# The second MoE's steps get a row count, six of them with a last tile of 64 rows, and attention by pairs starts two tiles later

## The chip, the cores and the metric

The kernel runs on one core of a Trainium2 chip. The metric is the device time of one execution in microseconds (us). TensorE (PE) multiplies matrices, VectorE (DVE) and ScalarE (ACT) work on tiles, GpSimd (POOL) does so too and issues the indirect transfers, SyncE (SP) issues the other transfers. PEld in a profile is PE's loading of the stationary operand.

## The reference

Chunked attention over 4 x 768 positions with 8 heads of 64, a dense gated MLP (called the first MoE here), and a top-1 mixture of 8 experts, all in float32:

```python
# attention: chunks of 32 queries, 16 positions of context to the left, 8 to the right, 8 memory slots
scores = scale * np.matmul(q_c, k_full.transpose(0, 1, 3, 2))
a = softmax(scores)
out[:, :, c_start:c_end] = np.matmul(a, v_full)
# first MoE: 3072 tokens x 512, d_ff 1536
g = x @ w_gate
x = silu(g) * (x @ w_val) @ w_out
# second MoE: w1 [8, 512, 1024], w2 [8, 1024, 512]
logits = x @ w_gate
e_idx = np.argmax(logits, axis=1)
for e in range(E):
    mask = e_idx == e
    h = np.maximum(x[mask] @ w1[e], 0.0)
    out[mask] = gate_w[mask, None] * eom[mask, e, None] * (h @ w2[e])
```

## The kernel before

Attention runs in 48 tiles of 64 queries. A list of pieces (`attention_pieces`) is dealt out over slots between the matmuls of the first MoE's first token groups, one group of 384 tokens for every six tiles. A single tile (`at_S`) adds the mask on PE, by a matmul with an identity (L354), then multiplies 128 query columns at a time with 96 keys (L357); DVE only takes the maximum. A pair of tiles (`at_S2`) multiplies 64 x 64 blocks (L386), DVE adds the mask to both halves (L391) and takes the maximum (L392); ACT then takes the exponentials of 16 heads in a row (L395). Tiles below `PAIRED` are single, the rest run in pairs. While this goes on, DVE also converts the first MoE's weights from their 64-bit form (L226 to L231).

The first MoE keeps 8 groups of 384 tokens times 12 slices of d_ff; every f32 factor is split into a high and a low half in fp32r (a reduced f32 that PE multiplies in one pass), and three products replace one. After each group its tokens are routed: logits, expert, position in the expert's table (`posi`), and a scatter of the token's number into the table.

The second MoE runs in steps. A step takes one expert and two or three tiles of 128 tokens. It goes through 8 chunks of the expert's weights, 128 of the 1024 hidden columns each. Per chunk, `split_chunk` makes the high and low halves (ACT the cast, DVE one half of the low part and POOL the other, L889: tiles `wh`/`wl` and `gvh`/`gvl` in turn), `mm1` runs twelve matmuls into `g` with the tokens as moving operand (L947), DVE and ACT make the two halves of `h` (L951, L953), and a chunk later `mm2` runs three matmuls per tile into `o` (L969), with 128 columns of `h` as the stationary operand and 512 output columns moving. `gather` fetches a step's tokens by index (L916), `prep_x` transposes them on PE (L934), `evac_y` scales the result and `scatter_y` writes it to the tokens' rows (L985).

Three steps come first, for experts 0, 1 and 2 and known beforehand. What the other steps take is computed on the chip by `make_schedule`: a generator on DVE over tiny rows of one partition (8 experts, 19 slots, 8 x 19 products), run piece by piece by `later(delay, ...)` at ticks of a clock that counts two ticks per chunk. Then follow five steps of three tiles and four of two, always run, and up to ten more of two tiles that run only if the schedule asks for them (`tc.If`). At chunk `ready` the first dynamic transfers are issued.

Of the kernel before, what the change touches and what calls it, by code (L numbers as in the profile page):

```python
# [21 lines left out]
def tile_chunk_attention_moe_moe2(  # L22
# [16 lines left out]
    nc = tc.nc  # L39
# [26 lines left out]
    NTRI = 5  # L66
    NPAIR = 14
    NPU = 4
    NCV = 6
    PAIRED = 2 * GU  # L70
    NSP = 31
    WARM = 10
    LOADS = "w0 q0 q1 q2 w1 v0 v1 q3 w2 q4 w3 w4 v2 w5 q5 v3 v4 v5"
# [662 lines left out]
        nc.vector.tensor_scalar(out=out_, in0=a, scalar1=s1, scalar2=s2, op0=op0, **kw)  # L736

    def row(tag, shape=(1, E), dtype=F32):
        return sm.tile(list(shape), dtype, tag=tag, name=tag)

    def stt(out_, a, s1, b, op0, op1):
        nc.vector.scalar_tensor_tensor(out=out_, in0=a, scalar=s1, in1=b, op0=op0, op1=op1)

    def make_schedule():
        NS = NTRI + NPAIR

        def over_slots(vec, n):
# [22 lines left out]
        stt(tri_, hf, 1.0, odd, ALU.is_ge, ALU.mult)  # L770
        m8 = row("m8", (1, E, E))
        tt(m8, over_slots(tri_, E), upto, ALU.mult)
        tcum = total(m8, E, "tcum")
        yield
        stt(tri_, tcum, float(NTRI), tri_, ALU.is_le, ALU.mult)
        ts(tcum, tcum, float(NTRI), ALU.min)
# [16 lines left out]
        gt = row("gt", (1, NTRI, E))
        tt(gt, over_slots(tcum, NTRI), over_experts(sidx[:, 0:NTRI], NTRI), ALU.is_le)
        te = total(gt, NTRI, "te")
        tt(pk, pk, skip, ALU.subtract)
        ts(pk, pk, 1.0, ALU.add, float(2 * P), ALU.mult)
        stt(pk, pe, float(ES), pk, ALU.mult, ALU.add)
# [3 lines left out]
        tt(gt, over_experts(te, NTRI), over_slots(sidx[:, 0:E], NTRI), ALU.is_equal)  # L802
        tt(gt, gt, over_slots(trow, NTRI), ALU.mult)
        tst = total(gt, NTRI, "tst")
        stt(pk[:, 0:NTRI], te, float(E), pk[:, 0:NTRI], ALU.is_ge, ALU.mult)
        stt(te, te, float(E), te, ALU.is_lt, ALU.mult)
        tt(pe[:, 0:NTRI], pe[:, 0:NTRI], te, ALU.add)
        yield
        stt(pk[:, 0:NTRI], tst, -2.0 * P, pk[:, 0:NTRI], ALU.add, ALU.max)
        ts(sched_i[:, 1, 0:NS], pk, float((E - 1) * ES + N), ALU.min)  # L810
        ts(sched_i[:, 0, 0:NS], pe, float(E - 1), ALU.min)
        tt(used, used, pcum[:, E - 1:E], ALU.add)
        ts(sched_i[:, 0, NS:NS + 1], used, float(NTRI), ALU.subtract, 0.0, ALU.max)


    steps = [(e, 2) for e in range(NEARLY)] + [(None, 3)] * NTRI + [(None, 2)] * NPAIR
# [357 lines left out]
```

## Time and profile before

| what | value |
| --- | --- |
| median of three runs | 1165.75 us (1165.01 to 1165.78) |
| profiled execution | 1161.31 us, span 1159.6 us |
| PE busy | 1112.3 us, 96% of the span |
| weight loads (PEld) busy | 992.8 us, 86% |
| DVE / ACT / POOL busy | 592.7 / 597.7 / 674.1 us |
| mean granted clock of TensorE | 0.984 of full |

A busy time is the sum of an engine's instructions; overlapping ones count once. Matmuls are pipelined: the length shown for one is longer than the distance from its start to that of the next, and the distance is what it costs. The table is one profiled execution; the median belongs to other executions.

### The profile page before, as it was taken

How to read it: one execution, taken by the hardware profiler on the slowest of the kernel's cores; microseconds unless marked ns; L12 is line 12 of the kernel's file. 1: busy time of each engine (PE TensorE's matmuls, PEld its weight loads, DVE VectorE, ACT ScalarE, POOL GpSimd, SP SyncE). 2: the span in 40 equal slices, each digit the busy share in tenths (PEclk: the TensorE clock that was granted, in tenths of full speed). 3: DMA queues.
4: the chain of work that ended last, by engine and by line, in shares of the span. 5: the costliest groups of instructions: out<-in, count | busy, mean ns of one | idle time of the engine just before them, and what ended most of it. 6: DMA issues, size and time to landing. Idle time of an engine off the chain costs nothing.

```text
span 1159.6 us, 20391 instructions
## 1 busy us (share of the span) xinstructions
PE 1112.3 (96%) x7458; PEld 992.8 (86%) x7458; DVE 592.7 (51%) x1167; ACT 597.7 (52%) x1300; POOL 674.1 (58%) x459
## 2 busy tenths in 40 slices
PE   7789899999999999999999999999999999999994
PEld 5678788898998998899899899888789998998994
DVE  6699844444444544544444443425884344444541
ACT  5678755545555556555554554444454434334551
POOL 4589854554654554555365565566666555566773
PEclk7799999999999999999999999999999999999998
DMA  9777524211211211221210100265169444546673
GB/s 207 193 196 214 165 59 124 53 27 36 63 37 37 60 42 29 52 49 29 58 40 18 38 12 19 67 125 173 64 213 324 157 147 158 171 156 197 206 227 123
DMA packets 204959, 126.55 MB, mean 109 GB/s; under 512 B 110960, under 2 KB 181744, under 8 KB 204850
## 3 DMA queue, kind: packets, MB, share of 16 engines
q1 hardware_dynamic: 199282, 110.70, 35.3%
q0 software_dynamic: 5568, 14.45, 3.6%
q8 instruction: 61, 1.00, 0.4%
q14 instruction: 48, 0.39, 0.2%
HBM read 111.61 MB, written 14.82 MB: 109 GB/s over the span
## 4 chain that ended last, share of the span: by engine, by line
PE 80%; DVE 6%; issue 4%; POOL 3%; SPq 2%; DMA 2%; ACT 2%; POOLq 0%; ACTq 0%; DVEq 0%
PE ps_g L530 32%; PE acc L571 15%; PE g L947 11%; PE o L969 11%; PE ps_pv L433 2%; PE ps_t L325 2%; PE ps_att L416 2%; SPq L274 1%; PE ps_att L386 1%; PE ps_x L616 1%; PE a L934 1%; DVE ps_c L228 1%; DVE ps_c L226 1%; PE ps_l L626 1%; DVE w L231 1%
## 5 line engine op out<-in xcount | busy, mean ns | idle before, releaser
L180 POOL TENSOR_TENSOR gvl<-w,gvh 128x1024 fp32r<-128x1024 f32 x96 | 233.1, 2429 | 89.9 <-ACT gvh L179 66.7
L530 PE MATMUL ps_g<-xh,gvh 128*128 128x384 f32 x768 | 271.7, 354 | 0.6 <-ACT gvh L179 0.6
L530 PE MATMUL ps_g<-xh,gvl 128*128 128x384 f32 x768 | 261.4, 340 | 3.5 <-POOL gvl L180 3.5
L530 PE MATMUL ps_g<-xl,gvh 128*128 128x384 f32 x768 | 261.5, 340 | 0.0
L180 POOL TENSOR_TENSOR ol<-w,oh 128x512 fp32r<-128x512 f32 x96 | 124.7, 1299 | 201.6 <-ACT oh L179 201.5
L571 PE MATMUL acc<-oh,h 128*128 128x512 f32 x576 | 202.9, 406 | 0.9 <-DVE h L560 0.9
L543 DVE SCALAR_TENSOR_TENSOR th<-th,ps_g 128x384 f32<-128x384 f32 x96 | 53.0, 552 | 194.1 <-ACT th L538 194.1
L530 PEld LDWEIGHTS ps_g<-xh,gvh 128*128 128x128 f32 x768 | 145.5, 189 | 5.2 <-ACT gvh L179 0.8
L530 PEld LDWEIGHTS ps_g<-xh,gvl 128*128 128x128 f32 x768 | 145.1, 189 | 4.5 <-POOL gvl L180 4.5
L530 PEld LDWEIGHTS ps_g<-xl,gvh 128*128 128x128 f32 x768 | 145.5, 189 | 1.8
L554 ACT CAST h<-th 128x384 fp32r<-128x384 f32 x96 | 49.1, 512 | 166.8 <-DVE th L552 166.7
L571 PEld LDWEIGHTS acc<-oh,h 128*128 128x128 f32 x576 | 108.1, 188 | 25.8 <-issue 1.4
L951 ACT ACTIVATE h<-g 128x256 fp32r<-128x256 f32 (+1 forms) x96 | 41.3, 430 | 160.4 <-PE g L947 151.4
L571 PE MATMUL acc<-ol,h 128*128 128x512 f32 x288 | 113.7, 395 | 0.3 <-POOL ol L180 0.3
L953 DVE SCALAR_TENSOR_TENSOR h<-g,h 128x256 fp32r<-128x256 f32 (+1 forms) x96 | 45.8, 477 | 118.3 <-ACT h L951 97.2
L560 DVE TENSOR_TENSOR h<-th,h 128x384 fp32r<-128x384 f32 x96 | 81.0, 844 | 39.1 <-ACT h L554 38.5
L179 ACT CAST gvh<-w 128x1024 fp32r<-128x1024 f32 x96 | 100.4, 1046 | 1.1 <-POOL w L234 1.1
L538 ACT ACTIVATE th<-ps_g 128x384 f32<-128x384 f32 x96 | 47.0, 490 | 92.8 <-PE ps_g L530 92.6
L552 DVE TENSOR_TENSOR th<-th,ps_g 128x384 f32<-128x384 f32 x96 | 53.0, 552 | 64.6 <-PE ps_g L530 64.0
L969 PE MATMUL o<-gvh,h 128*128 128x512 f32 x232 | 80.9, 397 | 1.6 <-DVE h L953 1.6
L969 PE MATMUL o<-wh,h 128*128 128x512 f32 x232 | 80.4, 394 | 0.0
L889 POOL TENSOR_TENSOR wl<-w,wh 128x512 fp32r<-128x512 f32 x30 | 50.6, 1690 | 37.6 <-ACT wh L887 37.1
(196 smaller groups left out, 2299.8 us busy)
## 6 DMA issues: line engine op xcount, KB each, us to landing
w<-in_moe_w_dram SPq DMA_DIRECT2D x120, 256.0 KB
ra<-in_moe_w_dram SPq DMA_DIRECT2D x72, 256.0 KB
kt<-in_k_dram SPq DMA_DIRECT2D x35, 176.0 KB
vt<-in_v_dram SPq DMA_DIRECT2D x35, 176.0 KB
xs<-xr SPq DMA_DIRECT2D x8, 769.5 KB
st<-in_moe_w_gate_dram SPq DMA_DIRECT2D x12, 512.0 KB
st<-in_moe_w_val_dram SPq DMA_DIRECT2D x12, 512.0 KB
st<-in_moe_w_out_dram SPq DMA_DIRECT2D x12, 512.0 KB
```

Of the source, the lines that this page charges most:

```text
L179: nc.scalar.copy(out=hi, in_=src)
L180: lo_eng.tensor_tensor(out=lo, in0=src, in1=hi.bitcast(F32), op=ALU.subtract)
L530: nc.tensor.matmul(ps, a[:, c], x[:, kk, :], start=(n == 0), stop=(n == 3 * KD - 1))
L538: nc.scalar.activation(out=th, in_=ps, func=AF.Tanh, scale=0.5)
L543: nc.vector.scalar_tensor_tensor(out=th, in0=th, scalar=1.0, in1=ps, op0=ALU.add, op1=ALU.mult)
L552: nc.vector.tensor_tensor(out=hh, in0=hh, in1=ps, op=ALU.mult)
L554: nc.scalar.copy(out=h1, in_=hh)
L560: nc.vector.tensor_tensor(out=h2, in0=hh, in1=h1.bitcast(F32), op=ALU.subtract)
L571: nc.tensor.matmul(accs[g][j], a[:, c], w_, start=(f == 0 and n == 0), stop=(f == NF - 1 and n == 2))
L889: eng.tensor_tensor(out=b[:, i], in0=r[:, i], in1=a[:, i].bitcast(F32), op=ALU.subtract)
L947: nc.tensor.matmul(ps, wx[:, 0, c * P:(c + 1) * P], xx[:, c, :], start=(i == 0), stop=(i == 3 * KD - 1))
L969: nc.tensor.matmul(ysd[s][t], hx[:, c], wx[:, 1], start=(j == 0 and i == 0), stop=(j == NFE - 1 and i == 2))
```

## The change

Steps carry a row count. After the three early steps come two three-tile steps with 384 rows, three with 320, one two-tile step with 256 and three with 192; the conditional ones keep 256. In the six narrow steps the last tile has 64 rows: its gather, transposes, scaling and scatter take 64, `mm1` has 320 or 192 moving columns, and `mm2` for that tile loads 64 stationary columns and still moves 512. `make_schedule` decides by the number of leftover blocks of 64 which expert's rest goes to a wide or a narrow step. It has 14 pieces in place of 7, one per tick in place of every second; `ready` goes from 14 to 15. Its row tiles have one buffer in place of two. `PAIRED` goes from 12 to 14.

```diff
     NPU = 4
+    NTW = 2
+    NPW = 1
     NCV = 6
-    PAIRED = 2 * GU
+    PAIRED = 2 * GU + 2
...
     def row(tag, shape=(1, E), dtype=F32):
-        return sm.tile(list(shape), dtype, tag=tag, name=tag)
+        return sm.tile(list(shape), dtype, tag=tag, name=tag, bufs=1)
...
+        def running(vec, tag):
+            m8 = row("m8", (1, E, E))
+            tt(m8, over_slots(vec, E), upto, ALU.mult)
+            return total(m8, E, tag)
...
-        hall, odd = hof[:, 0, :], hof[:, 1, :]
+        hall, odd, half = hof[:, 0, :], hof[:, 1, :], hof[:, 2, :]
         yield
+
         hf = row("hf")
         tt(hf, hall, early1, ALU.subtract)
+        t5 = row("t5")
+        stt(t5, hf, 1.0, odd, ALU.is_ge, ALU.mult)
+        t6 = row("t6")
+        tt(t6, t5, half, ALU.mult)
+        tt(t5, t5, t6, ALU.subtract)
+        c6 = running(t6, "c6")
...
+        ts(li, li, 1.0, ALU.add, float(2 * P), ALU.mult)
+        stt(li, le, float(ES), li, ALU.mult, ALU.add)
+        ge = row("ge", (1, NS, E))
+        tt(ge, over_slots(scum, NS), over_experts(si, NS), ALU.is_le)
+        se = total(ge, NS, "sse")
+        srow = row("srow")
+        tt(srow, hall, odd, ALU.add)
+        ts(srow, srow, 1.0, ALU.subtract, float(2 * P), ALU.mult)
+        tt(srow, srow, ebase[0:1, 0, :], ALU.add)
+        yield
+        ge = row("ge", (1, NS, E))
+        tt(ge, over_experts(se, NS), over_slots(sidx[:, 0:E], NS), ALU.is_equal)
+        tt(ge, ge, over_slots(srow, NS), ALU.mult)
+        pk = total(ge, NS, "pk")
+        off = row("off", (1, NS))
+        ts(off, se, float(E), ALU.is_ge, float(E * ES), ALU.mult)
+        tt(pk, pk, off, ALU.add)
+        yield
...
+        ts(sched_i[:, 1, 0:NS], pk, float((E - 1) * ES + N), ALU.min, 0.0, ALU.max)
+        ts(sched_i[:, 0, 0:NS], se, float(E - 1), ALU.min)
+        tt(b1, b1, scum[:, last], ALU.add)
+        ts(b1, b1, float(M), ALU.subtract)
+        tt(b0, lcum[:, last], lc, ALU.subtract)
+        tt(b1, b1, b0, ALU.max)
+        ts(sched_i[:, 0, NS:NS + 1], b1, float(NPU), ALU.add)
+
+
+    HALF = P // 2
+    steps = ([(e, 2, 2 * P) for e in range(NEARLY)]
+             + [(None, 3, 3 * P)] * NTW + [(None, 3, 3 * P - HALF)] * (NTRI - NTW)
+             + [(None, 2, 2 * P)] * NPW + [(None, 2, 2 * P - HALF)] * (NPU - NPW)
+             + [(None, 2, 2 * P)] * (NPAIR - NPU))
+
+    def rows(s, t):
+        return min(P, steps[s][2] - t * P)
...
         for t in range(steps[s][1]):
+            r = rows(s, t)
             nc.gpsimd.indirect_dma_start(
-                out=x[:, t, :], out_offset=None, in_=xs,
-                in_offset=bass.IndirectOffsetOnAxis(ap=idx[:, t:t + 1], axis=0))
+                out=x[0:r, t, :], out_offset=None, in_=xs,
+                in_offset=bass.IndirectOffsetOnAxis(ap=idx[0:r, t:t + 1], axis=0))
...
             sc = m2_tile(s, "sc")
-            nc.vector.tensor_copy(sc[:, 0:nt], x[:, 0:nt, DM:XW])
+            full = steps[s][2] // P
+            nc.vector.tensor_copy(sc[:, 0:full], x[:, 0:full, DM:XW])
+            if full < nt:
+                nc.vector.tensor_copy(sc[0:HALF, full:nt], x[0:HALF, full:nt, DM:XW])
...
         for c in range(KD):
-            nc.tensor.transpose(ps[:, c, :], x[:, t, c * P:(c + 1) * P], ident)
-        c_ = slice(t * P, (t + 1) * P)
-        hi_lo(ps, th[:, :, c_], tl[:, :, c_], nc.vector)
+            nc.tensor.transpose(
+                ps[:, c, 0:r], x[0:r, t, c * P:(c + 1) * P], ident[0:r, 0:r])
+        c_ = slice(t * P, t * P + r)
+        hi_lo(ps[:, :, 0:r], th[:, :, c_], tl[:, :, c_], nc.vector)
 
     def mm1(n):
         s = n // NFE
-        w = steps[s][1] * P
+        w = steps[s][2]
...
         for t in range(nt):
-            c = slice(t * P, (t + 1) * P)
+            r = rows(s, t)
+            c = slice(t * P, t * P + r)
             for i, (hx, wx) in enumerate(((h1, a), (h1, b), (h2, a))):
-                nc.tensor.matmul(ysd[s][t], hx[:, c], wx[:, 1],
+                nc.tensor.matmul(ysd[s][t][0:r], hx[:, c], wx[:, 1],
 
...
-        for i in range(7):
-            later(13 + 2 * i, next, sched, None)
+        for i in range(14):
+            later(13 + i, next, sched, None)
         nextc = NRA + NF
-        ready = 14
+        ready = 15
```

On DVE, in the second MoE between one `w*l` (the low half of a weight chunk) and the next `h`, the fourth gap of the schedule held six small instructions; `m`, `pk`, `te`, `trow` and the others are rows of the schedule. Before:

```order
L889 TENSOR_TENSOR wl<-w,wh 128x512
L640 TENSOR_TENSOR gt<-tcum,sidx 1x40
L643 TENSOR_REDUCE te<-gt 1x5
L640 TENSOR_TENSOR pk<-pk,skip 1x19
L736 TENSOR_SCALAR pk<-pk 1x19
L742 SCALAR_TENSOR_TENSOR pk<-pe,pk 1x19
L742 SCALAR_TENSOR_TENSOR trow<-hof,ebase 1x8
L953 SCALAR_TENSOR_TENSOR h_9396<-g,h_9394 128x256
```

The same gap of the changed kernel, without the `wl` ahead and the `h` behind:

```order
L738 TENSOR_SCALAR li<-li 1x19
L744 SCALAR_TENSOR_TENSOR li<-le,li 1x19
L642 TENSOR_TENSOR ge<-scum,si 1x152
L645 TENSOR_REDUCE sse<-ge 1x19
L642 TENSOR_TENSOR srow<-hof 1x8
L738 TENSOR_SCALAR srow<-srow 1x8
L642 TENSOR_TENSOR srow<-srow,ebase 1x8
L642 TENSOR_TENSOR ge<-sse,sidx 1x152
L642 TENSOR_TENSOR ge<-ge,srow 1x152
L645 TENSOR_REDUCE pk<-ge 1x19
L738 TENSOR_SCALAR off<-sse 1x19
L642 TENSOR_TENSOR pk<-pk,off 1x19
```

Six small instructions became twelve, five of them over 152 products. Over the whole schedule, 37 DVE instructions became 85; the six gaps between successive `h` that held 4, 6, 6, 6, 6 and 5 hold 13, 18, 12, 12, 13 and 12, and the first piece, ahead of them, has 5 in place of 4.

On PE, in a three-tile step, `g` is the first layer's result and `o` the second's; `xh` is a half of the tokens, `wh`, `wl` and `gvh` are halves of the weights, and `h_...` those of the hidden values. Before, from the end of one tile's `o` over the last tile's three to the next chunk's first `g`:

```order
L969 MATMUL o<-wh,h_10610 128x512
L969 MATMUL o<-wh,h_10608 128x512
L969 MATMUL o<-wl,h_10608 128x512
L969 MATMUL o<-wh,h_10610 128x512
L947 MATMUL g<-xh,gvh 128x384
```

Of the change, in the first narrow three-tile step:

```order
L1057 MATMUL o<-wh,h_10674 128x512
L1057 MATMUL o<-wh,h_10672 64x512
L1057 MATMUL o<-wl,h_10672 64x512
L1057 MATMUL o<-wh,h_10674 64x512
L1034 MATMUL g<-xh,gvh 128x320
```

The `g` matmuls have 320 columns in place of 384; the last three of `o` write 64 rows in place of 128, with 512 columns as before.

On PE, in the first token group, where attention's pair of tiles 12 and 13 stood between the first MoE's second layer (`acc`) and its first (`ps_g`). Before:

```order
L571 MATMUL acc_768<-oh,h_1473 128x512
L386 MATMUL ps_att<-kT,qbd_115 64x96 x16
L325 MATMUL ps_t<-ident,qt 128x128 x4
L530 MATMUL ps_g<-xh,gvh 128x384
```

Of the change, tile 12 alone, 22 rows earlier in PE's order (tile 13 follows 61 rows later):

```order
L435 MATMUL ps_pv<-pT,vt 64x64 x8
L356 LDWEIGHTS identb
L356 MATMUL ps_att<-masks,identb 128x384
L359 MATMUL ps_att<-kT,qbd_115 128x96 x4
L532 MATMUL ps_g<-xh,gvh 128x384
```

One run of 16 small score matmuls (64x96) became two runs of a mask matmul and four score matmuls (128x96), apart from each other and the first of them earlier. On DVE the two mask additions of L391 for these tiles are gone.

## Rows read from the trace of the kernel before

**Rows 1.** The page, part 4: the chain that ended last, by engine.

```profile
PE 80%; DVE 6%; issue 4%; POOL 3%; SPq 2%; DMA 2%; ACT 2%; POOLq 0%; ACTq 0%; DVEq 0%
```

**Rows 2.** Busy time by stretch; columns PE, PEld, DVE, ACT, POOL, clock, DMA, GB/s.

```profile
86.00:150.00 64.00, 56.34 (x401) 49.06 (x400) 57.68 (x107) 49.53 (x111) 53.18 (x38) 1.00 0.61 178
...
820.00:850.00 30.00, 25.91 (x169) 22.36 (x168) 27.72 (x75) 15.09 (x25) 17.50 (x14) 1.00 0.13 45
...
1064.00:1145.00 81.00, 80.75 (x521) 72.51 (x519) 39.78 (x67) 40.75 (x64) 57.30 (x40) 1.00 0.69 220
```

**Rows 3.** Waits of PE, 820 to 865 us: total, times, longest.

```profile
PE g L947 <- DVE wl L889: 2.5, 2, 1.6
PE o L969 <- DVE h L953: 1.6, 1, 1.6
```

**Rows 4.** Timeline of DVE through the scheduling: start us, us, instruction.

```profile
828.11 2.40 DVE L889 TENSOR_TENSOR wl<-w,wh 128x512 fp32r<-128x512 f32 x1
830.43 0.15 DVE L640 TENSOR_TENSOR hf<-hof,early 1x8 f32<-1x8 f32 x1
830.61 0.15 DVE L742 SCALAR_TENSOR_TENSOR tri__9250<-hf,hof 1x8 f32<-1x8 f32 x1
830.80 0.21 DVE L640 TENSOR_TENSOR m<-tri__9250,upto 1x64 f32<-1x64 f32 x1
...
831.52 0.67 DVE L889 TENSOR_TENSOR gvl<-w,gvh 128x512 fp32r<-128x512 f32 x1
...
834.06 1.25 DVE L736 TENSOR_SCALAR pk<-sidx,tcum 1x19 f32<-1x19 f32 x1
...
835.35 0.30 DVE L640 TENSOR_TENSOR ge<-pcum,pk 1x152 f32<-1x152 f32 x1
...
837.85 1.99 DVE L640 TENSOR_TENSOR pk<-pk,skip 1x19 f32<-1x19 f32 x1
839.87 0.16 DVE L736 TENSOR_SCALAR pk<-pk 1x19 f32<-1x19 f32 x1
```

**Rows 5.** Timeline of POOL in the same stretch.

```profile
838.45 1.35 POOL L889 TENSOR_TENSOR wl<-w,wh 128x512 fp32r<-128x512 f32 x1
```

**Rows 6.** Timeline of PE, the twelve L947 matmuls of a three-tile chunk.

```profile
911.18 0.34 PE L947 MATMUL g<-xh,wh 128*128 128x384 f32 x1
...
913.27 0.39 PE L969 MATMUL o<-gvh,h 128*128 128x512 f32 x1
```

**Rows 7.** Timeline of PE, ten L947 matmuls of a two-tile chunk.

```profile
1097.75 0.28 PE L947 MATMUL g<-xh,wl 128*128 128x256 f32 x1
...
1098.89 0.40 PE L969 MATMUL o<-gvh,h 128*128 128x512 f32 x1
```

**Rows 8.** Timeline of PE, scores of one single attention tile.

```profile
57.79 0.33 PE L354 MATMUL ps_att<-masks,identb 128*128 128x384 bf16 x1
57.96 1.02 PE L357 MATMUL ps_att<-kT,qbd 128*128 128x96 f32 x8
58.77 0.42 PE L530 MATMUL ps_g<-xh,gvh 128*128 128x384 f32 x1
```

**Rows 9.** Timeline of PE at the first transposes of the fourth step.

```profile
867.25 0.60 PE L934 MATMUL a<-ident,xg 128*128 128x128 f32 x4
867.60 0.37 PE L947 MATMUL g<-xh,wh 128*128 128x256 f32 x1
```

**Rows 10.** Timeline of PE, scores of a later pair.

```profile
164.28 0.89 PE L386 MATMUL ps_att<-kT,qbd 64*64 64x96 f32 x32
```

**Rows 11.** Waits of PE, 126 to 152 us, four of six lines.

```profile
PE ps_att L386 <- DVE w L231: 1.1, 1, 1.1
PE ps_t L325 <- ACT s L395: 1.0, 1, 1.0
PE acc L571 <- DVE h L560: 0.9, 1, 0.9
PE ps_t L325 <- DVE s L391: 0.7, 1, 0.7
...
```

More of the change, by code (lines that the diff above doesn't have):

```diff
@@ L745, in make_schedule @@
         NS = NTRI + NPAIR
+        M = NTRI + NPU
         def over_slots(vec, n):
@@ L756, in total @@
             return y.rearrange("o s e -> o (s e)")
+        def running(vec, tag):
+            m8 = row("m8", (1, E, E))
+            tt(m8, over_slots(vec, E), upto, ALU.mult)
+            return total(m8, E, tag)
+        last = slice(E - 1, E)
         xi = row("xi", dtype=I32)
         stt(xi, base[0:1, 0, :], float(P - 1), ebase[0:1, 0, :], ALU.add, ALU.subtract)
-        ho = row("ho", (1, 2, E), I32)
+        ho = row("ho", (1, 3, E), I32)
         ts(ho[:, 0, :], xi, 8, ALU.arith_shift_right)
         ts(ho[:, 1, :], xi, 7, ALU.arith_shift_right, 1, ALU.bitwise_and)
-        hof = row("hof", (1, 2, E))
+        ts(ho[:, 2, :], xi, 6, ALU.arith_shift_right, 1, ALU.bitwise_and)
+        hof = row("hof", (1, 3, E))
         nc.vector.tensor_copy(hof, ho)
-        hall, odd = hof[:, 0, :], hof[:, 1, :]
+        hall, odd, half = hof[:, 0, :], hof[:, 1, :], hof[:, 2, :]
         yield
@@ L768, in make_schedule @@
         tt(hf, hall, early1, ALU.subtract)
-        tri_ = row("tri_")
[L770 to L776, printed above, removed]
+        t5 = row("t5")
[5 more added lines that the diff above has]
+        yield
+        stt(t6, c6, float(NTW), t6, ALU.is_le, ALU.mult)
+        n6 = row("n6", (1, 1))
+        ts(n6, c6[:, last], float(NTW), ALU.min)
+        c5 = running(t5, "c5")
+        ts(c5, c5, n6, ALU.add)
+        stt(t5, c5, float(NTRI), t5, ALU.is_le, ALU.mult)
+        used = row("used", (1, 1))
+        ts(used, c5[:, last], float(NTRI), ALU.min)
+        yield
+        rk = row("rk")
+        tt(c6, c6, t6, ALU.mult)
+        tt(rk, c5, t5, ALU.mult)
+        tt(rk, rk, c6, ALU.add)
+        tri_ = row("tri_")
+        tt(tri_, t5, t6, ALU.add)
         p = row("p")
@@ L779, in make_schedule @@
         tt(p, p, hf, ALU.add)
-        tt(m8, over_slots(p, E), upto, ALU.mult)
-        pcum = total(m8, E, "pcum")
+        sh = row("sh")
+        stt(sh, odd, 1.0, half, ALU.subtract, ALU.mult)
+        stt(sh, sh, 1.0, tri_, ALU.add, ALU.subtract)
+        tt(p, p, sh, ALU.subtract)
         yield
-        used = tcum[:, E - 1:E]
-        pk = row("pk", (1, NS))
-        ts(pk, sidx[:, 0:NS], used, ALU.subtract)
+        lcum = running(p, "lcum")
+        scum = running(sh, "scum")
+        q_ = row("q_", (1, 4))
@@ new lines, in make_schedule @@
+        lc, al, b0, b1 = (q_[:, i:i + 1] for i in range(4))
+        ts(lc, used, -1.0, ALU.mult, float(NTRI + NPW), ALU.add)
+        tt(lc, lc, lcum[:, last], ALU.min)
+        tt(b0, used, lc, ALU.add)
+        tt(b1, used, lcum[:, last], ALU.add)
+        ts(al, lc, float(M), ALU.subtract)
+        yield
+        li = row("li", (1, NS))
+        ts(li[:, 0:M], sidx[:, 0:M], used, ALU.subtract)
+        ts(li[:, M:NS], sidx[:, M:NS], al, ALU.add)
+        si = row("si", (1, NS))
+        ts(si[:, 0:M], sidx[:, 0:M], b0, ALU.subtract)
@@ L786, in make_schedule @@
+        ts(si[:, M:NS], sidx[:, M:NS], b1, ALU.subtract)
+        isl = row("isl", (1, NS))
+        ts(isl[:, 0:M], li[:, 0:M], lc, ALU.is_lt)
+        ts(isl[:, M:NS], li[:, M:NS], lcum[:, last], ALU.is_lt)
+        yield
         tt(p[:, NEARLY - 1:NEARLY], p[:, NEARLY - 1:NEARLY], sidx[:, 1:2], ALU.add)
         ge = row("ge", (1, NS, E))
-        tt(ge, over_slots(pcum, NS), over_experts(pk, NS), ALU.is_le)
-        pe = total(ge, NS, "pe")
+        tt(ge, over_slots(lcum, NS), over_experts(li, NS), ALU.is_le)
@@ L790, in make_schedule @@
+        le = total(ge, NS, "le")
         tt(ge, ge, over_slots(p, NS), ALU.mult)
         skip = total(ge, NS, "skip")
+        tt(li, li, skip, ALU.subtract)
         yield
[L793 to L798, printed above, removed]
+        ts(li, li, 1.0, ALU.add, float(2 * P), ALU.mult)
@@ new lines, in make_schedule @@
+        stt(li, le, float(ES), li, ALU.mult, ALU.add)
[6 more added lines that the diff above has]
+        tt(srow, srow, ebase[0:1, 0, :], ALU.add)
+        yield
+        ge = row("ge", (1, NS, E))
+        tt(ge, over_experts(se, NS), over_slots(sidx[:, 0:E], NS), ALU.is_equal)
@@ L799, in make_schedule @@
+        tt(ge, ge, over_slots(srow, NS), ALU.mult)
[3 more added lines that the diff above has]
+        tt(pk, pk, off, ALU.add)
+        yield
+        tt(li, li, pk, ALU.subtract)
+        tt(li, li, isl, ALU.mult)
+        tt(pk, pk, li, ALU.add)
+        tt(le, le, se, ALU.subtract)
+        tt(le, le, isl, ALU.mult)
+        tt(se, se, le, ALU.add)
         trow = row("trow")
@@ L801, in make_schedule @@
         yield
[L802 to L807, printed above, removed]
+        g1 = row("g1", (1, NTRI, E))
+        tt(g1, over_slots(rk, NTRI), over_experts(sidx[:, 1:NTRI + 1], NTRI), ALU.is_equal)
+        any_ = total(g1, NTRI, "any_")
+        g2 = row("g2", (1, NTRI, E))
+        tt(g2, g1, over_slots(sidx[:, 0:E], NTRI), ALU.mult)
+        te = total(g2, NTRI, "te")
+        tt(g2, g1, over_slots(trow, NTRI), ALU.mult)
+        tst = total(g2, NTRI, "tst")
         yield
+        ts(any_, any_, -1.0, ALU.mult, 1.0, ALU.add)
+        tt(se[:, 0:NTRI], se[:, 0:NTRI], any_, ALU.mult)
+        tt(se[:, 0:NTRI], se[:, 0:NTRI], te, ALU.add)
+        tt(pk[:, 0:NTRI], pk[:, 0:NTRI], any_, ALU.mult)
         stt(pk[:, 0:NTRI], tst, -2.0 * P, pk[:, 0:NTRI], ALU.add, ALU.max)
[L810 to L816, printed above, removed]
+        yield
+        ts(sched_i[:, 1, 0:NS], pk, float((E - 1) * ES + N), ALU.min, 0.0, ALU.max)
[12 more added lines that the diff above has]
+        return min(P, steps[s][2] - t * P)
     NSTEP = len(steps)
@@ L895, in load_idx @@
             return
-        e, nt = steps[s]
+        e, nt = steps[s][:2]
         idx = m2_tile(s, "idx")
@@ L926, in prep_x @@
         if t == 0:
-            xgT[s] = [m2_tile(s, g, [P, KD, nt * P]) for g in ("xh", "xl")]
+            xgT[s] = [m2_tile(s, g, [P, KD, steps[s][2]]) for g in ("xh", "xl")]
             sc = m2_tile(s, "sc")
-            nc.vector.tensor_copy(sc[:, 0:nt], x[:, 0:nt, DM:XW])
+            full = steps[s][2] // P
+            nc.vector.tensor_copy(sc[:, 0:full], x[:, 0:full, DM:XW])
+            if full < nt:
+                nc.vector.tensor_copy(sc[0:HALF, full:nt], x[0:HALF, full:nt, DM:XW])
             xgs[s] = (x, idx, sc)
@@ L966, in mm2 @@
         for t in range(nt):
-            c = slice(t * P, (t + 1) * P)
+            r = rows(s, t)
+            c = slice(t * P, t * P + r)
             for i, (hx, wx) in enumerate(((h1, a), (h1, b), (h2, a))):
-                nc.tensor.matmul(ysd[s][t], hx[:, c], wx[:, 1],
+                nc.tensor.matmul(ysd[s][t][0:r], hx[:, c], wx[:, 1],
                                  start=(j == 0 and i == 0), stop=(j == NFE - 1 and i == 2))
@@ L976, in evac_y, with scatter_y @@
             yo = m2_tile(s, "yo")
+            r = rows(s, t)
             if t == 1 or s == 0:
-                nc.scalar.activation(out=yo, in_=ys[t], func=AF.Copy, scale=sc[:, t, :])
+                nc.scalar.activation(out=yo[0:r], in_=ys[t][0:r], func=AF.Copy, scale=sc[0:r, t, :])
             else:
                 nc.vector.tensor_scalar(
-                    out=yo, in0=ys[t], scalar1=sc[:, t, :], scalar2=None, op0=ALU.mult)
-            later(1 + 2 * t, scatter_y, yo, idx, t)
-    def scatter_y(yo, idx, t):
+                    out=yo[0:r], in0=ys[t][0:r], scalar1=sc[0:r, t, :], scalar2=None, op0=ALU.mult)
+            later(1 + 2 * t, scatter_y, yo, idx, t, r)
+    def scatter_y(yo, idx, t, r):
         sc = nc.gpsimd.indirect_dma_start(
-            out=out, out_offset=bass.IndirectOffsetOnAxis(ap=idx[:, t:t + 1], axis=0),
-            in_=yo, in_offset=None, bounds_check=N - 1, oob_is_err=False)
+            out=out, out_offset=bass.IndirectOffsetOnAxis(ap=idx[0:r, t:t + 1], axis=0),
+            in_=yo[0:r], in_offset=None, bounds_check=N - 1, oob_is_err=False)
         independent(sc, t, "the tiles of a step hold different tokens")
```

## The prediction

> **What bounds the kernel now.** I read the chain that ended last first: 80% of it is TensorE (PE), 6% VectorE (DVE) [rows 1]. So a saved PE instruction is worth its spacing to the next one, except where PE waits. The table by stretch says where it waits [rows 2]: while attention goes over to pairs (86 to 150 us) PE is busy 56.34 of 64 us and DVE 57.68; while the schedule of the second MoE is made (820 to 850 us) PE is busy 25.91 of 30 and DVE 27.72; in the two-tile steps at the end (1064 to 1145 us) PE is busy 80.75 of 81. The change touches all three. In the second stretch every wait of PE is for DVE: 2.5 us for `wl`, 1.6 us for `h` [rows 3]. DVE there runs long `w*l` and `h` instructions with the small schedule instructions between them, without a pause, and some take far longer than others of their kind: a `wl` 2.40 us where a `gvl` of its shape took 0.67; a 19-wide `pk` 1.25 and 1.99 us where another took 0.16 [rows 4]. The 1.99 us one ends at 839.84, where a POOL subtraction ends (838.45 + 1.35 = 839.80) [rows 5]. In this stretch DVE sets the pace.
>
> **The change part by part.** Profiled, the kernel took 1161.31 us (span 1159.6), 4.44 below the median of the runs, 1165.75. The sum is made against the first and then moved to the second.
>
> *Three-tile steps of 320 rows.* Twelve `g` matmuls of 384 columns start 911.18 to 913.27, 0.174 us each [rows 6]; of 256 columns ten start in 1097.75 to 1098.89, 0.114 each [rows 7]. That is 0.060 us per 128 columns, so 64 columns fewer save 0.030. 3 steps x 8 chunks x 12 = 288 matmuls: -8.6 us. The second layer's matmuls of the last tile load 64 instead of 128 columns of `h`, but still stream 512: nothing.
>
> *Two-tile steps of 192 rows.* Also 288 matmuls, and a straight line would give 0.084 us each, again -8.6. But each needs its own load of 128 weight columns, which overlaps the matmul before. The nearest rows with a small moving side are the attention scores: eight matmuls with 128-column f32 weights and only 96 moving columns fill 57.96 to 58.77, 0.101 us each [rows 8]. So the floor lies near 0.10 to 0.11, hardly below the 0.114 of today. I take 0.108: 0.006 x 288 = -1.7 us, with bounds -8.6 (no floor) and 0. The Trainium skill says the same from its side: "TensorE: Matmul & The Clock Gate", LDWEIGHTS (loading the stationary operand), gives the columns divided by 1.2 in ns, 107 ns for 128, and by that these steps would save 0.007 x 288 = 2.0 us, not 8.6. It is a rule that speaks against this half of the change; the scores' 0.101 lie 6% under it.
>
> *Transposes.* Four of 128 rows take 867.25 to 867.60, 0.35 us [rows 9]. Six tiles now have 64 rows: half of that, 0.17 x 6 = 1.0, if the columns count, 0 if the load of 128 columns does. I take -0.5. The last scatter moves 64 rows, not 128: -0.2, a guess between 0 and half of one 1 us POOL issue, such as the other indirect ones.
>
> *Schedule.* From 37 DVE instructions to 85 (counted in the order). By width, the 48 added are 25 of up to 8 elements, 13 of 19 (or its two halves), 5 of 152, 4 of 64, 1 of 40. Rows: 0.15, 0.16, 0.30, 0.21 and, between the last two sorts, 0.19; a dependent one starts 0.03 after the end of the one before it (830.43 + 0.15 to 830.61), an independent one overlaps [rows 4]. Spacings of 0.14, 0.15, 0.335, 0.22 and 0.22 give 3.5 + 1.95 + 1.68 + 0.88 + 0.22 = 8.2 us. Nothing hides it where DVE sets the pace; queued behind the pieces stand the `h` and `w*l` that PE waits for. About 1.0 us (seven small instructions) falls into the last gap, after PE's last wait, where DVE has room again: +7.2 us. That the first dynamic weights are asked for a chunk later costs nothing that I can see: the first use is nine chunks after the request. The gather of the first three-tile step moves by a chunk too; its transposes ran without a wait at 867.25 [rows 9], so its margin is not shown: 0 to 2 us, taken 0.
>
> *Attention.* Tiles 12 and 13 go singly. A pair's scores, 32 small matmuls, take 0.89 us where nothing holds them [rows 10]; a single tile takes 0.98 us (57.79 to 58.77, its mask first [rows 8]), so two take 1.1 us of PE more. For it DVE loses two mask additions, and the eight-head softmax falls in two halves, not one run. PE's waits in that stretch that name the pair's own instructions or DVE's conversion are 1.1, 1.0, 0.9 and 0.7 us [rows 11], 3.7 in all. Bounds: +1.1 (all waits remain) and -2.6 (all go: 3.7 - 1.1), and more if the conversion gets ahead; since DVE remains as busy as PE until 150 us, half of the best case and a little: -2.0.
>
> Sum: -8.6 - 1.7 - 0.5 - 0.2 + 7.2 - 2.0 = -5.8. That is 1155.5 us on the profiled run's scale, 1160.0 on the median's.
>
> **The rivals.**
> *The narrow two-tile steps follow the line.* Then 288 x 0.030 instead of 1.7: 6.9 more, 1153.1. For it: the score matmuls are f32 and not fp32r; against it: their weights have the same size.
> *DVE's pieces only fill its waits for POOL.* Three long instructions hold 1.73 + 1.09 + 1.83 = 4.7 us beyond their kind [rows 4]. If the added instructions run while POOL has the port, DVE comes to its next long one when POOL is done, and the cost falls to 7.2 - 4.7 = 2.5 us: 1155.3. Against it: PE's order of chunks feeds POOL too, so POOL's work moves back with DVE's.
> *They meet POOL more often (slower).* Now six gaps have 12 to 18 instructions, and each that starts beside a POOL subtraction can wait up to 1.35 us [rows 5]. If every gap takes one more such wait of 1.0 us, 6 more are lost: 1166.0; from 3.6 us of further waits on, the gain is under the bound below. For it: the waits are there already; against it: of the 37 small instructions only two were held long. The Trainium skill has this as an exclusive lock on a shared port pair of DVE and GpSimd ("SBUF — State Buffer", Who interferes with whom); by that rule the sign is open, since whichever engine comes first holds off the other, and the rows agree that the waits end with POOL's instruction.
> *A moving side under 256 columns runs in two passes,* as the f32 score matmuls do (4 in the order, 8 in the trace [rows 8]). No fp32r matmul below 256 is in the trace. Each would cost 2 x 0.11: (0.22 - 0.114) x 288 = +30 us, 1190.
> *The slots don't fit the tokens.* Then a conditional two-tile step is run: 96 matmuls of 0.114 us and 48 of 512 columns, by the same slope 0.234 each, 22 us: 1182. By the inputs the experts get 539, 588, 408, 438, 350, 192, 269 and 288 tokens; experts 0, 1 and 2 have 256 of them in early pairs. What is left of 1 and 4 (332, 350) fits the two wide triples, of 0, 6 and 7 (283, 269, 288) the narrow ones; expert 3 takes the wide pair and a narrow one (256 + 182), and 2 and 5 (152, 192) the other narrow ones. All 12 steps are used and none is over, but expert 5 fits to the token.
>
> **How the numbers follow.** Chances: my sum 0.60; no floor 0.13; absorbed 0.11; more meetings 0.09; two passes 0.05; a tail step 0.02. About 0.2%, 2.3 us, is what a measurement here can tell from no change. My sum's own range is 1156.5 to 1163.5 (schedule 5 to 9.5, attention +1.1 to -3); a tenth of it ends within the bound. So faster: 0.54 + 0.13 + 0.11 = 0.78; same: 0.06 + 0.03 = 0.09; slower: 0.06 of the meetings, two passes, tail step = 0.13. The range goes down to the no-floor case, 1152.5, and up to 1164.0; outside lie most of the meetings, the last two cases and a little of the first two, 0.18.
>
> **What would show it.** `g` matmuls of 320 columns start every 0.144 us and of 192 every 0.108; at 0.084, or at 0.2, a rival holds. DVE busy without a pause through some 34 us where it was 27, PE waiting some 11 us in this stretch instead of 4.1, all for `w*l` and `h`. No 128x256 step after the last pair. Fewer and shorter waits of PE at 126 to 150 us. My forecast is wrong if the schedule's pieces cost under 4 or over 11 us: it is the one term large enough to turn the sign, and the one where a wait's length hangs on which engine comes first.

## The result, and the profile after

The changed kernel takes 1154.54 us (median of 4 runs, 1153.4 to 1155.73), the kernel before 1165.62. The ratio is 0.9913, with a 95% interval of 0.9894 to 0.9931: 11.1 us faster, where 5.8 were forecast. The two profiled executions are only 7.0 us apart in span (1159.6 and 1152.6), because the one of before, 1161.31 us, ran faster than any of its 4 timed runs; its first `acc` matmul (the first MoE's second layer) starts at 60.96 us, and that of the changed kernel, with nothing changed ahead of it, at 63.48.

The table by stretch of the changed kernel, with the columns of [rows 2]:

```profile
86.00:150.00 64.00, 58.62 (x389) 51.75 (x390) 58.25 (x105) 51.31 (x118) 56.53 (x41) 1.00 0.66 187
820.00:850.00 30.00, 24.72 (x130) 21.03 (x129) 28.31 (x102) 11.11 (x17) 15.76 (x13) 0.83 0.13 45
1064.00:1137.00 73.00, 73.00 (x481) 61.41 (x479) 32.21 (x62) 35.13 (x57) 51.62 (x37) 1.00 0.69 217
```

In the first stretch PE is busy 58.62 us of 64, 2.3 more than before, with about the same of DVE. In the second PE does less and DVE more, and the granted clock falls to 0.83: for two parts of this stretch, 10 us in all, it stood at half of full (1.2 of 2.4 GHz), each time behind a wait of PE of 1.7 or 1.8 us for DVE's `h`. The third is full.

The waits of PE around the schedule, 815 to 865 us, against [rows 3]:

```profile
PE o L1057 <- DVE h L1040: 4.8, 4, 1.8
PE g L1034 <- DVE gvl L970: 0.8, 1, 0.8
PE g L1034 <- DVE wl L970: 0.4, 1, 0.4
```

They make 6.0 us in place of 4.1, while the second MoE's first 16 chunks take 6.4 us longer than before. The other half of that is in PE's own matmuls at the lower clock: the `g` and `o` of these chunks take 48.0 us, start to start, where they took 44.8.

The waits of PE in 126 to 152 us (line, what released it, total us, times, longest), against [rows 11]:

```profile
PE ps_pv L435 <- ACT kT L318: 1.3, 1, 1.3
PE ps_t L327 <- DVE w L233: 0.6, 1, 0.6
PE ps_att L418 <- issue: 0.3, 1, 0.3
```

Of six waits, 4.6 us in all, three with 2.2 us are left. The four of [rows 11] (3.7 us) are gone; that for ACT's copy of `kT` has grown from 0.5 to 1.3 us, and one of 0.6 us for the `w` of DVE's conversion has come in another place.

PE's timeline in a narrow three-tile chunk, at a narrow step's last transposes, and in a narrow two-tile chunk:

```profile
948.17 0.31 PE L1034 MATMUL g<-xh,wh 128*128 128x320 f32 x1
...
949.92 0.40 PE L1057 MATMUL o<-gvh,h 128*128 128x512 f32 x1
...
1008.39 0.46 PE L1020 MATMUL a<-ident,xg 64*128 64x64 f32 x4
1008.78 0.42 PE L1034 MATMUL g<-xh,gvh 128*128 128x320 f32 x1
...
1068.30 0.25 PE L1034 MATMUL g<-xh,wh 128*128 128x192 f32 x1
...
1069.62 0.42 PE L1057 MATMUL o<-gvh,h 128*128 128x512 f32 x1
```

Twelve `g` matmuls of 320 columns take 1.75 us, 0.146 each ([rows 6]: 0.174), twelve of 192 take 1.32, 0.110 each ([rows 7]: 0.114). The four transposes of 64 rows take 0.39 us, not less than the 0.35 of 128 rows in [rows 9].

DVE's timeline in the scheduling, the instructions that were held and took over 1 us, with one that was not held between them:

```profile
824.15 2.32 DVE L970 TENSOR_TENSOR wl<-w,wh 128x512 fp32r<-128x512 f32 x1
...
828.87 0.67 DVE L970 TENSOR_TENSOR gvl<-w,gvh 128x512 fp32r<-128x512 f32 x1
...
830.45 1.17 DVE L744 SCALAR_TENSOR_TENSOR sh<-sh,tri__9290 1x8 f32<-1x8 f32 x1
...
833.62 2.29 DVE L970 TENSOR_TENSOR gvl<-w,gvh 128x512 fp32r<-128x512 f32 x1
...
839.92 1.27 DVE L642 TENSOR_TENSOR srow<-hof 1x8 f32<-1x8 f32 x1
...
844.51 1.26 DVE L642 TENSOR_TENSOR sse<-sse,le 1x19 f32<-1x19 f32 x1
...
847.80 1.24 DVE L738 TENSOR_SCALAR any__9463<-any__9463 1x5 f32<-1x5 f32 x1
```

POOL's subtractions at the same times:

```profile
830.32 1.28 POOL L970 TENSOR_TENSOR gvl<-w,gvh 128x512 fp32r<-128x512 f32 x1 [2.97 <-ACT gvh L968]
...
839.91 1.26 POOL L970 TENSOR_TENSOR wl<-w,wh 128x512 fp32r<-128x512 f32 x1 [3.11 <-ACT wh L968]
844.46 1.28 POOL L970 TENSOR_TENSOR gvl<-w,gvh 128x512 fp32r<-128x512 f32 x1 [3.28 <-ACT gvh L968]
847.69 1.33 POOL L970 TENSOR_TENSOR gvl<-w,gvh 128x512 fp32r<-128x512 f32 x1 [1.95 <-ACT gvh L968]
```

Each of the four small instructions that was held starts 0.01 to 0.13 us behind one of these and ends within 0.03 us of its end. All six of DVE, beyond their kind, hold 1.65 + 1.02 + 1.62 + 1.12 + 1.10 + 1.09 = 7.6 us. Before, the three of [rows 4] held 4.7 and a `wl` of 3.50 us at 840.57 another 2.8: 7.5 us (a `gvl` of 1.32 us at 847.51, behind the last piece, is left out). The waits fall on other instructions, but their sum is about the same; in the five other kernels below with the same schedule it is 6.7 to 7.1 us.

Line by line down PE's order the two executions part as follows (the same matmul in both, changed minus before): 63.48 - 60.96 = +2.5 at the start; -0.2 at 203 us, behind attention; -4.0 at the second MoE's first chunk (794.99 and 798.96); +2.5 at its 17th (855.35 and 852.88); +2.1 at its 41st, where the narrow three-tile steps begin (948.17 and 946.06); -5.8 at its 65th (1044.44 and 1050.26); -7.4 at the last matmul (1136.96 and 1144.35); -7.0 at the end. So attention's stretch gave 2.7, the stretch of the first MoE where nothing was changed 3.8, the schedule took 6.4, the narrow three-tile steps gave 7.9, the two-tile ones 1.6. Of the 3.8 us, 0.9 are a wait of PE for POOL's `gvl` near 780 us, 2.54 us long in one execution and 1.60 in the other; over all the profiles of this document it is 1.3 to 3.8 us, at the same place of `xh` too, so it is not put down to the change.

### The profile page after: what moved, and what is told of

Read it like the earlier page. It is cut to its first block, busy times and chain, and to the rows that moved or that the text cites. A ratio compares the mean times of both kernels' runs of the same rounds, so it can differ in the third digit from the quotient of the medians.

```text
span 1152.6 us, 20408 instructions
## 1 busy us (share of the span) xinstructions
PE 1107.3 (96%) x7444; PEld 978.1 (85%) x7444; DVE 600.1 (52%) x1219; ACT 593.4 (51%) x1301; POOL 668.8 (58%) x459
## 4 chain that ended last, share of the span: by engine, by line
PE 63%; issue 15%; POOL 8%; DVE 5%; DMA 4%; SPq 3%; ACT 2%; POOLq 0%; ACTq 0%
PE ps_g L532 32%; PE acc L573 16%; PE g L1034 3%; PE o L1057 2%; PE ps_pv L435 2%; POOL gvl L970 2%; PE ps_t L327 2%; POOL out_dram L1074 2%; PE ps_att L418 2%; SPq L276 2%; POOL wl L970 1%; PE ps_att L388 1%; PE ps_x L618 1%; DMA st<-in_moe_w_gate_dram 1%; DMA st<-in_moe_w_val_dram 1%
## 5 line engine op out<-in xcount | busy, mean ns | idle before, releaser
L1038 ACT ACTIVATE h<-g 128x256 fp32r<-128x256 f32 (+3 forms) x96 | 38.6, 402 | 159.2 <-PE g L1034 133.6
L562 DVE TENSOR_TENSOR h<-th,h 128x384 fp32r<-128x384 f32 x96 | 88.8, 925 | 39.1 <-ACT h L556 39.1
L1040 DVE SCALAR_TENSOR_TENSOR h<-g,h 128x256 fp32r<-128x256 f32 (+3 forms) x96 | 42.7, 445 | 112.0 <-ACT h L1038 98.5
L1057 PE MATMUL o<-wh,h 128*128 128x512 f32 (+1 forms) x232 | 81.2, 398 | 3.0 <-DVE h L1040 3.0
L1057 PE MATMUL o<-gvh,h 128*128 128x512 f32 (+1 forms) x232 | 82.0, 402 | 1.8 <-DVE h L1040 1.8
```

Source lines behind the costliest of these rows:

```text
L562: nc.vector.tensor_tensor(out=h2, in0=hh, in1=h1.bitcast(F32), op=ALU.subtract)
L1040: nc.vector.scalar_tensor_tensor(out=h2, in0=ps, scalar=0.0, in1=h1.bitcast(F32), op0=ALU.max, op1=ALU.subtract)
L1057: nc.tensor.matmul(ysd[s][t][0:r], hx[:, c], wx[:, 1], start=(j == 0 and i == 0), stop=(j == NFE - 1 and i == 2))
```

## The experiments

Each was timed beside the kernel before, whose medians were 1164.64 us (the first four), 1166.14 (the next four) and 1166.4 (the last three); its single runs lie between 1161.8 and 1169.0. So ratios are compared.

**Attention alone**, in the kernel before:

```diff
-    PAIRED = 2 * GU
+    PAIRED = 2 * GU + 2
```

> The kernel before with attention's pairs from tile 14 on and nothing else. Theory: this alone gave about 3.1 us, since in the two profiles the changed kernel loses 2.5 us against the other up to 110 us and stands level or ahead from 150 us on; 1162.5 against 1165.6. Rival: the two profiles only had different starts, and attention gives nothing or the 1.1 us that PE has more to do: 1165.6 to 1166.7.

1161.65 us, ratio 0.9968 (0.9953 to 0.9983): 3.7 us, between 2 and 5.5. In its profile the distance from the first `acc` matmul to the 145th is 2.0 us shorter than before. Its waits of PE in 100 to 165 us:

```profile
PE ps_t L325 <- DVE w L231: 1.3, 2, 0.6
PE ps_pv L433 <- ACT kT L316: 1.3, 1, 1.3
PE ps_att L416 <- issue: 0.7, 2, 0.5
PE ps_att L354 <- DVE w L231: 0.5, 1, 0.5
```

The gain is attention's own; "nothing" is out. This kernel's token tiles lie where those of the kernel before do, so the effect of the next two runs is not in it.

**The row tiles' buffers alone**, in the kernel before:

```diff
     def row(tag, shape=(1, E), dtype=F32):
-        return sm.tile(list(shape), dtype, tag=tag, name=tag)
+        return sm.tile(list(shape), dtype, tag=tag, name=tag, bufs=1)
```

> The kernel before with one buffer in place of two for the schedule's row tiles, and nothing else: no instruction of it changes, only where tiles lie in SBUF. Theory: the 175 instead of 177 ns that the first MoE's matmuls of 384 columns take in the changed kernel come from where the tiles lie, so this gives 2 to 3 us, spread evenly over 160 to 790 us: 1163. Rival: the 2 ns are a difference of executions, or come from something else: 1165.6, and the spacing stays at 177.

1161.54 us, ratio 0.9967 (0.9951 to 0.9984): 3.8 us (1.9 to 5.7) for a line that was costed at nothing. The smaller pool lets the tiles behind it, the token halves `xh` and `xl` first, start 1728 bytes lower.

**The same with the place given back**, an unused tile of 1728 bytes:

```diff
     sm = ctx.enter_context(tc.tile_pool(name="sm", bufs=2))
+    pad = sm.tile([P, 432], F32, tag="pad", name="pad", bufs=1)
+    nc.gpsimd.memset(pad[0:1, 0:1], 0.0)
```

> The row tiles with one buffer as in e2_row_buffers, and an unused tile of 1728 bytes per partition behind them, so that the first MoE's token tiles lie again at 144768 as in the kernel before, and not at 143040. Theory, place: the gain is lost, 1164.6, and the 384-column matmuls start every 177 ns again. Rival, the buffers themselves (fewer tiles, other waits): 1161.5 and 173 ns stay.

1165.68 us, ratio 0.9996 (0.9984 to 1.0009). The gain is gone: it was the place, not the buffers. PE's timeline over the same 24 matmuls of the first MoE, first of the kernel before (`xh` at byte 144768 of a partition), then of the row buffers alone (143040), then with the place given back (144768), then of the changed kernel (144096):

```profile
400.16 0.44 PE L530 MATMUL ps_g<-xh,gvh 128*128 128x384 f32 x1
...
404.50 0.60 PE L416 MATMUL ps_att<-ident,s 128*96 128x128 f32 x4
```

```profile
400.61 0.44 PE L530 MATMUL ps_g<-xh,gvh 128*128 128x384 f32 x1
...
404.88 0.38 PE L416 MATMUL ps_att<-ident,s 128*96 128x128 f32 x2
```

```profile
402.05 0.44 PE L532 MATMUL ps_g<-xh,gvh 128*128 128x384 f32 x1
...
406.40 0.60 PE L418 MATMUL ps_att<-ident,s 128*96 128x128 f32 x4
```

```profile
399.00 0.44 PE L532 MATMUL ps_g<-xh,gvh 128*128 128x384 f32 x1
...
403.30 0.60 PE L418 MATMUL ps_att<-ident,s 128*96 128x128 f32 x4
```

4.34, 4.27, 4.35 and 4.30 us. Over the whole first MoE such matmuls in a row start every 176.6, 173.6, 176.6 and 174.9 ns on average. There are 2304 of them: 1.7 ns x 2304 = 3.9 us between before and the change. Of these, 1872 or 3.2 us lie in the stretch behind 203 us where the two profiles part by 3.8, and with the 0.9 us of the wait for `gvl` taken off that, 2.9 are left, which the place accounts for.

The row buffers alone would gain 3.0 x 2304 = 6.9 us by the same count, more than their timed interval allows, so a part of it is lost again. Where is not settled. In the profiled execution PE waited 3.8 us for that `gvl`, and the granted clock fell to half behind it; six of the 13 profiles show such a fall there, those of before and of the change not.

**The changed kernel at the old place**: the same lines with 168 elements, which puts `xh` at 144768.

> The changed kernel with 672 bytes of unused tile, so that the token tiles lie at 144768 as in the kernel before, not at 144096. Theory, place: 177 ns in place of 175 for the first MoE's 1,900 matmuls between the stretches that wait, 2 to 3 us lost: 1157. Rival: the change does not owe anything to the place: 1154.5.

1157.7 us, ratio 0.9933 (0.9916 to 0.9951), against 0.9913 of the change: 2.3 us, 3.2 by the medians. The spacing is 176.6 ns again. The two intervals overlap; together with the spacing's 3.9 us, some 2 to 4 us of the 11 come from the place. This is also the kernel that the prediction's sum describes, with the place as before: 7.8 us faster than before, 5.7 to 9.8. **And at another one**, with 120 elements, 144576:

> The changed kernel with 480 bytes of unused tile, which moves the token tiles from 144096 (an odd multiple of 32) to 144576 (an odd multiple of 64). Theory, place: 173 to 174 in place of 175 ns, about 2 us: 1152.5. Rival: no difference, 1154.5.

1153.93 us, ratio 0.9908 (0.9893 to 0.9923): the spacing went to 173.6 ns as expected, the time cannot be told from the change's, so the 2 us expected are not shown.

**The steps without attention**, the changed kernel with `PAIRED = 2 * GU`:

> The changed kernel with pairs from tile 12 on, as before: the steps and the schedule alone. Theory: attention's 3.1 us are lost again, 1157.6, and the 2 us of the first MoE's matmuls stay. Rival: attention gave nothing, 1154.5.

1157.69 us, ratio 0.9931 (0.9909 to 0.9952): 2.1 us slower than the change by the ratios, 3.1 by the medians.

**Full widths with the new schedule**:

```diff
-             + [(None, 3, 3 * P)] * NTW + [(None, 3, 3 * P - HALF)] * (NTRI - NTW)
-             + [(None, 2, 2 * P)] * NPW + [(None, 2, 2 * P - HALF)] * (NPU - NPW)
+             + [(None, 3, 3 * P)] * NTW + [(None, 3, 3 * P)] * (NTRI - NTW)
+             + [(None, 2, 2 * P)] * NPW + [(None, 2, 2 * P)] * (NPU - NPW)
```

> The changed kernel with its schedule of 14 pieces, but with every step at its full 384 or 256 rows. It shows the narrow widths' gain, and what is left beside it. Theory: the 320-column matmuls save 28 ns each and the 192-column ones 5, 288 of each: 8.1 + 1.5 us, so 1164.2. Rival, no floor by the weight loads: 8.1 + 8.6, 1171.2.

1164.07 us, ratio 0.9988 (0.9974 to 1.0003). The widths are worth 0.0075 of 1165, 8.7 us, 9.5 by the medians; 17 is out. What is left beside them, attention and the place together some 6 us, is nearly eaten by the schedule: from the ninth chunk to the 17th this kernel takes 34.14 us, the changed one 34.89, the one before 28.29. In this run the stretch kept its clock:

```profile
820.00:850.00 30.00, 21.12 (x128) 16.75 (x127) 28.24 (x109) 11.76 (x18) 16.11 (x13) 1.00 0.14 45
```

Its waits of PE, 815 to 870 us:

```profile
PE o L1057 <- DVE h L1040: 8.1, 7, 2.9
PE g L1034 <- DVE wl L970: 0.7, 1, 0.7
```

DVE is as busy as in the changed kernel (28.31) and the chunks take as long but for 0.75 us, with the clock at 1.00 in place of 0.83: where DVE sets the pace, the lower clock costs at most that, and PE's waits are shorter where its matmuls take longer. What brings the fall is not shown: this run waited longer, 8.8 us against 6.0, and kept its clock. Four more kernels with this schedule, profiled for the other experiments here, take 34.14 to 34.21 us for these chunks and four with the old one 28.29 to 28.92: the schedule costs 5.2 to 5.9 us, and the 34.89 are the odd ones.

**No narrow two-tile steps**, and so a schedule of 51 instructions in 13 pieces (the schedule's parts for `sh`, `scum`, `si`, `isl`, `sse`, `srow` go, the pairs are placed as before):

```diff
-             + [(None, 2, 2 * P)] * NPW + [(None, 2, 2 * P - HALF)] * (NPU - NPW)
-             + [(None, 2, 2 * P)] * (NPAIR - NPU))
+             + [(None, 2, 2 * P)] * NPAIR)
...
-        for i in range(14):
+        for i in range(13):
             later(13 + i, next, sched, None)
         nextc = NRA + NF
-        ready = 15
+        ready = 14
```

> The changed kernel with narrow three-tile steps alone: two-tile steps at 256 rows, and a schedule that no longer sorts them, 51 DVE instructions in 13 pieces where it has 85 in 14. Theory, DVE sets the pace and each instruction costs about 0.15 us: 34 fewer give 5.1 us, the pairs' 320 ns per chunk lose 1.5, so 1151.0. Rival, the schedule's price is waiting for POOL and not the count of instructions: it stays, and only the 1.5 us are lost, 1156. The place of the token tiles (143488) may add or take 1 to 2 us; it is read from the spacing of the 384-column matmuls.

1154.55 us, ratio 0.9911 (0.9897 to 0.9925), no faster than the change, and 176.6 ns in the first MoE: the place, 143488 (3.9 us by the spacing), and the pairs' full width took back what the schedule gave. From the ninth chunk to the 17th it takes 31.45 us, 3.4 less than the change, where 5.1 were expected. **The same with 16 elements of padding**, `xh` at 143552:

> e6_no_narrow_pairs with 64 bytes of unused tile, which puts the token tiles at 143552. Theory, place: like 143040 and unlike 144768 this is an odd multiple of 64, so spacing 173 to 174 ns and about 3 us less than e6 if that one has 177. Rival, the place within 128 bytes does not matter: same as e6 within 1 us.

1149.25 us, ratio 0.9865 (0.9849 to 0.9882): faster than the kernel before and than the changed one, and the intervals do not touch. It is 5.3 us under the run before it, where about 3 were expected. The spacing is 173.6 ns, and the eight chunks take 30.00 us. Its waits of PE around the schedule, against [rows 3] and the change's 6.0 us:

```profile
PE o L1013 <- DVE h L996: 2.4, 2, 1.8
PE g L990 <- DVE wl L926: 0.7, 1, 0.7
```

**A last tile of 32 rows** in that kernel's three narrow steps:

```diff
-    HALF = P // 2
+    HALF = 96
+    LAST = P - HALF
...
-        ts(ho[:, 2, :], xi, 6, ALU.arith_shift_right, 1, ALU.bitwise_and)
+        ts(ho[:, 2, :], xi, 5, ALU.arith_shift_right, 3, ALU.bitwise_and)
...
-        tt(t6, t5, half, ALU.mult)
+        stt(t6, half, 1.0, t5, ALU.is_ge, ALU.mult)
```

> e7_no_narrow_pairs_padded with a last tile of 32 rows in the three narrow steps, 288 columns in place of 320 (the rests of 283, 269 and 288 tokens just fit). Theory, a three-tile step is bound by PE's columns: 14 ns x 288 = 4.0 us, 1145.2. Rival, at chunks of 3.7 us another engine or the 118 ns floor holds PE: about 1149.2.

1147.46 us, ratio 0.9843 (0.9825 to 0.9861), the fastest of all; the step from the one before it is 2.6 us by the ratios and its interval overlaps. The twelve matmuls of 288 columns:

```profile
944.55 0.30 PE L991 MATMUL g<-xh,wh 128*128 128x288 f32 x1
...
946.01 0.29 PE L991 MATMUL g<-xh,wl 128*128 128x288 f32 x1
```

Eleven spacings fill 1.46 us, 0.133 each, 13 ns under 320 columns. 0.013 x 288 = 3.7 us is within what the two intervals allow. The two profiles show it in the steps themselves: the three narrow ones (chunk 41 to 65) take 92.05 us, and 96.27 without the change, 4.2 us where 4.0 were expected. So these steps still shrink with their columns; the eight chunks of the schedule took 30.84 us in this execution, 0.84 more.

**Pairs from tile 16 on**, in the changed kernel (`PAIRED = 2 * GU + 4`, and `fast = i < 17`, so that tile 15 has its mask on PE too):

> The changed kernel with attention by pairs from tile 16 on (tiles 14 and 15 single too, with the mask on PE). Theory, the gain of tiles 12 and 13 came from DVE in the stretch to 150 us, where it is as busy as PE; behind it PE is full, so the further pair costs PE's 1.1 us: 1155.6. Rival, the single form is better anywhere in the first group: another 3 us, 1151.5.

1154.63 us, ratio 0.9898 (0.9883 to 0.9913): 0.1 us slower than the change by the medians, 1.7 faster by the ratios, so the times do not tell the two expectations apart. The profiles do, with one execution each: from the first `acc` matmul to the 289th this kernel takes 265.0 us, the changed one 263.0 and the one with full widths, whose attention is the same, 263.2. Some 2 us are lost there, so another 3 us of gain is out, and the loss is more than the 1.1 expected.

## Why the prediction was right, and where its sum was off

The sign and the range held; 1154.54 lies near the range's low end and 2 us under the forecast's own range. Some 2 to 4 us of the gain came from a term that the sum did not have, which was luck. Term by term:

- **Three-tile steps, -8.6.** The spacing came as forecast (0.146 us for 0.144), and 7.9 us between the profiles.
- **Two-tile steps, -1.7.** 0.110 us for 0.108, and 1.6 us. A floor is there, and "no floor" and "two passes" are both out; that it is the weight loads is inferred, for no run here takes the load away. The rule of the Trainium skill ("TensorE: Matmul & The Clock Gate", LDWEIGHTS (loading the stationary operand)) gives 107 ns; the measurement is 110 to 112. [rows 7] was one of the fast chunks: in the last 32 chunks before, the mean spacing runs from 114 to 127 ns, and in the run with full widths, at 144096, these chunks take 0.85 us less than before with the same matmuls. So the width itself is worth 0.7 us at that place and 1.3 in the changed kernel at the old one, and the rest of the 1.6 is the place.
- **Transposes, -0.5, and the last scatter, -0.2.** Nothing: 0.39 us for four transposes of 64 rows against 0.35 of 128 (97 and 89 ns each over all of them). The bound that I had given, "0 if the load of 128 columns does", was the right one; that it is the load is not shown. The last scatter took POOL 0.91 us, the one before it 1.00, and from the last matmul to the end the change takes 15.7 us, before 15.2.
- **Schedule, +7.2.** 6.4 us between the profiles, 5.2 to 5.9 with the five other kernels that have it. The 48 instructions cost 0.11 to 0.13 us each, for 0.15 in the sum: oversized by about 1 to 2 us. The reason for which it could have been otherwise, POOL, is seen in the timeline: six instructions are held in place of four, each for less, 7.6 us in place of 7.5. So neither "absorbed" nor "more meetings": the held time stays, or falls by less than 1 us, and the added instructions come on top. With 34 fewer instructions (31.45, 30.00 and 30.84 us in three kernels) 2.7 to 4.9 us came back, 0.08 to 0.14 each. Of the signs named, DVE without a pause came: 34.4 us, before 26.3. PE's waits did not: 6.0 us in place of some 11, and 8.8 in the run with full widths, whose clock did not fall.
- **Attention, -2.0.** 2.0 us in the profile of attention alone, 2.7 between the two profiles and in that of the changed kernel at the old place, 2.1 to 3.7 by the timed ratios: somewhat undersized. Of the waits named, all four went; the one for ACT's copy of `kT` grew to 1.3 us, and one for DVE's `w` (0.6) came.
- **What was missing.** The step that failed is one that the sum did not have: the row tiles' one buffer in place of two stood in the diff and got no price. It moves `xh` and `xl` by 672 bytes, and the first MoE's 384-column matmuls by 1.7 ns each: 3.9 us by the count, 2 to 4 us timed. With the unchanged stretch's 3.8 us (0.9 of them the wait for `gvl`) the profiles' parts are -7.9 - 1.6 + 6.4 - 2.7 - 3.8 = -9.6, inside the interval of the measured gain, 8.0 to 12.4. The rest of the 11.1 I leave open; it is less than the medians of the kernel before wander (1164.6 to 1166.4). At the old place, without this term, the sum's 5.8 met 7.8 us (5.7 to 9.8): that difference has the size of the oversized schedule.

The gather that moved by a chunk cost nothing that shows: from the 17th chunk to the 41st the change takes 92.8 us, before 93.2. No conditional step ran: both traces have 96 chunks.

The profile of before was also a poor zero: 4.3 us faster than its median. Its first `acc` matmul starts at 60.96 us; in the other 12 profiles, with nothing changed ahead of it, at 60.4 to 65.5, half of them past 62.6.

## What to carry to other kernels

Before a wide part of a step is trimmed, look at what floors the instruction: 64 columns off a 384-column matmul were worth 28 ns, off a 256-column one 4, and the second took 34 of the 48 instructions added to the scheduler; here leaving it out gave another 5 us (1149.25 against 1153.93 at like spacing). Bookkeeping on the engine that sets the pace costs most of its length (5.2 to 6.4 us of the 7.2 added up) even where each instruction is 0.15 us, and waits beside it absorb little of it. An edit that only changes how much memory a pool takes can move a tuned kernel by 0.3%: compare variants at the same place, or try a few.

## What the runs showed of the hardware that I had not expected

PE's speed on fp32r matmuls of 384 columns depends on where the moving tiles lie in a partition: 176.6 ns start to start, on average over the first MoE, with `xh` at byte 144768 (four kernels) and at 143488, 174.9 at 144096 (four kernels), 173.6 at 143040, 143552 (two kernels) and 144576. The first two are multiples of 128, the third is an odd multiple of 32, the last three odd multiples of 64. `gvh`, the stationary side, did not move. What in the chip does this was not tried; the other tiles behind `xh` (`xl` and the attention's) moved with it.
